# A retention recurrence and an MLP mixer on one core: four decay tables as steps of their own, a first decay held to land later in the plan, the maxima of the wide product allowed on two engines, and a new written-out order

## The chip, the cores and the metric

The kernel runs on one core of a Trainium2 chip. The metric is the device time of one execution in microseconds (us); the time before is the median of three executions. The engines are named as the profile names them: PE (matrix products; PEld is its weight load), DVE (vector), ACT (scalar), POOL and SP. POOL issues the loads, SP the transposes that are done by DMA, and SP and ACT the stores.

## What is computed

```python
def _attn_ref(q, k, v):                       # q, k, v: [4, 8, 768, 64]
    gamma = 1.0 - 2.0 ** (-5.0 - np.arange(H))
    for t in range(S):
        state = gamma * state + k[:, :, t] (outer) v[:, :, t]
        y[:, :, t] = scale * q[:, :, t] @ state

def _moe_ref(x, w_tok1, w_tok2, w_ch1, w_ch2):  # x: [4, 768, 512] = the heads side by side
    xt = x.transpose(0, 2, 1)
    h = np.maximum(xt @ w_tok1, 0.0) @ w_tok2   # 768 -> 256 -> 768
    u = x + h.transpose(0, 2, 1)
    h2 = np.maximum(u @ w_ch1, 0.0) @ w_ch2     # 512 -> 1536 -> 512
    return u + h2
```

## The kernel before

The work is cut by batch b (four) and, within a batch, by pair p of heads (four). `front(b, p)` does the recurrence and the token mixing of a pair; `back(b)` does the channel mixing of a batch.

A front works on six chunks of 128 positions. `decayed` multiplies k (and, for late pairs, q) by powers of the decay into `k16` and `q16`; there are two of these multiplies for a tile, one for each head, and each may go to ACT or DVE. `turn` transposes: mode "t" by PE (L348) with a copy to `kT` (L361), mode "w" by PE (L346) with a DVE multiply by the table `gq` into `qT` (L356), mode "x" by a DMA transpose from SP (L336). L377 makes the state products k'v, the chain of L387 and L389 scans them on DVE into `U`, and L398 or L401 scales the states into `r16`. L417 makes the scores k'q, L427 masks them on DVE (four times 384 wide for a pair), L438 and L447 add up y, L453 casts it. L467, L476 and L487 are the token mixing with the weights `wt1` and `wt2`; L493 casts u to fp16, L503 copies u to the tile `X`, and `uT` gets its transpose, by PE (L533, L540) in batch 0 and one pair of batch 1 and by a DMA transpose from SP (L517) otherwise.

`back` has two halves. Batches 0 and 1 widen plainly: L571 multiplies 384 positions at a time, and L587 takes the maximum while it leaves the bank. Batches 2 and 3 use a seven-product scheme (`widen7`): L612 makes sums of `uT`, L644 the products, L656 keeps partial sums on ACT, L661 adds on DVE, L682 and L690 take the maxima. L690 handles two 384-wide pieces at once in SBUF. All batches narrow with `narrow7`: L749 makes sums of the widened tiles, L785 and L795 are the products, L775 keeps, L802 adds into `X`, and the rows of `X` are stored (L832).

Tiles rotate through a few buffers: four each for the loads of q, k and v, and three for `X`, so batch 3's `X` takes the buffer of batch 0's.

The order is written out: nothing is scheduled when the kernel is built. The string PLAN names every step by two characters, in the order in which they are emitted; a further character chooses the engine where a step has several (`either`), and one the PSUM bank. `+n` stands for n products of a zero tile (L906) that fill PE. Each engine and each queue works its own steps in this order. The costs in the code (`act`, `dve`, and the pairs of numbers in `one` and `either`) served the search that wrote the string; at run time only the string counts.

The preparation makes tables: `gk` and `gy`, `ident16`, `gq` (four exponentials, one a pair, L222, in one step), `gs`, `gp` (on POOL, L232 and L234), `mask`. The first k tile, `(0, 0, "k")`, is called hard: it is loaded in fp32 by SP, not by POOL, and its two decay multiplies read fp32.

Of the kernel before, what the change touches and what calls it, by code (L numbers as in the profile page):

```python
# [9 lines left out]
F16 = mybir.dt.float16  # L10
# [11 lines left out]
class Op:  # L22
# [18 lines left out]
    "04050b000f010d0c0g03020e1h11i00907+e1n4061j51o1p1l10a2r01k11R01m+32v50i2w0h1q1r1s2s11S11u26+91v411x0j2t31T01w1"  # L41
    "U01V51z08+31A01W1y0l1X10k1Y2452260m1t01B1Z1D42u0+125651E31027+32x22820293203360n2y0p2z212A+23531C0340222B0q362"
    "C2F511F02a60r2302I2D0+22d32b2e0o2J2E251G12H1H2N51I02G2K22L3f712M02c11J1K01L01M2f12O3i3j1N12g73711O00s2P12h1P43"
    "8393a3H02i00z3b1Q03c2j0u2m2k03I2l03D12Q42n03n12R3e072S03E13h2p62T0t2W0x3F73d02U00y3g3k02q12o12V03l3o3G12X04f60"
    "v3m04g3p02Z33q43012Y03r0A3s14b03Q65273Rah33t3U3w4c0ae63S3T3u03z43x04d73B3A13J53C1af4e0agai4J13y03v13K4K13LaO4a"
    "R7aSaPaj3Man60E3NaQ3Y2ao4L0ak4aT3OaC53P10waDalapaEaU73V63WaV3Z4M1aW4P04h10B3X1400aI74iam0DaL54QaJ414424RaX34S0"
    "CaMaK4304T4U4j4kaYaZ441d451aF4aG47az7aN1baA460aw5191eaBat65h1axauaH4lbf4ay1fbg4mav5i00H1a1c4o10530I4804N6aq7ar"
    "4pbhbi4bjas4sb334904Obk4q5j14rb44W26045k14n0b07b654Y4t1b10Gb54V0bo504ub2bl6bp4Z4v0bmb74w34xbc7bn4z0151gbu64a4X"
    "4y0bvb84A164B0544b9555bd0F5Q0ba51252be4F4Cbs7bq1817bb5300Kbr4D0bKbt05704G0bO55604H00L4E05R0bxbwbLby158bz65n3bM"
    "5W15o5900PbP0bA0M5X5l0bB5a5T05p5YbT5U05ZbNbD5b06r05dbC0bU05m60bGbX5q5rbE61bH5V5e0ca65sc65f00S5Sc75u1043bY06s0c"  # L50
    "b1cc75yc2bV35vcd6o0c35x6p00JcfbQ55t05w5C05z4bWc8cg00O0N5A7u10R6t5D620bRbZc95B0c05c0cj5F7c15E0ck14I5G631523bS65"
    "645H0co5I5L5J06667ch55K1cp6870Q69ci6u26b45M06a06c5g5O36e16v6d16q6wclbF6f6x5N06y5P06g06zcT3cs6cmct6W1cU6kcu6B02"
    "51cV6E0Wc50cE66A1cF6D6X0d23d3cG6h7v0cN5cO6Fcv6cw7x10Td4db2cx6CcP6J16Z1cQ3bI0cR6G0cH5cScIdc6K6i16Hcecn6l16j0726"
    "c41dd7017A76Y6m0cy2cK3czcJ8A17y07Bd547CcL0V7D6I173cAd8571cr0dw2dxd60X7EcM7FcZ7d7dyd96L074cW3d00Yd17z6M2cX7w756"
    "N76da7G0dh4cB777cCdq6dr6O08B0781de5cYcDbJ0di820dk2dldjdf6Pdsdn7dCdt3dm0UdodpdudgdDdz4dA8318CdFdvdG2796735dEdBd"
    "H1dN46Q06n6S7c6T0dL6R17ddO7a6V7b6U0e23dM0dY850dRdP7e6dQ08D0dS7H01758E07fdU7g08617h47ie0847K0Ze97e307j07L7J7k11"
    "47P57Q7l7IeadVdTed877M07N7m113dZeee18827O08G17n8H7R0898F8a7q7o07r08b7S77T8c7p08I8J8de7dI67U08K7Y7s08LdJe80ek12"
    "el7Vem7W0eb8f41267Z0818i80011ec0eo77t8g7X0ep18jev58M0e44et8h8N0126e5enew8Re6egeh8Pez8k4ef8n68e0eu08QeA9b08l8oe"
    "x8m08Oeq38q18p08rey0eC9G08S0ercq18s09808T9H18teK39c0eG8u0eD8weY78V1eM5eL8x08WeBdKeHeZ8v08y0991eIeNeJes10eOf29M"
    "49e69I9Nf028U09f8Y58X08Zf1ePf3eR9gf5eQ2900eS9194f69O9h9ieW9PeT9j9Qfc9dff5eUf46920eXfgfa950fh3fj9k1fb9R9J1f7ft4"  # L60
    "fkfdf8fv79aej1960eVfu930fmfif9fwfnfl2fx9l0136frfyfA9K0fK7fBfLfo9ofsfpfHfz3fF9pfqg06fCfY5fZfO9n9mfDfPfIfM2g2fGg"
# [34 lines left out]
def kernel(  # L96
# [123 lines left out]
    def emit():  # L220
        for p in range(NP):
            nc.scalar.activation(gq[:, p], SINCE.tile.rearrange("p a b -> p (a b)")[:, :SH], AF.Exp, bias=lnsc, scale=lnh[:, p:p + 1])  # L222
# [716 lines left out]
```

## Time and profile before

| | |
|---|---|
| median of three executions | 187.66 us (187.24 to 189.37) |
| the profiled execution | 188.25 us, of it 186.5 us span from its first to its last instruction |
| busy, of the span | PE 178.7, DVE 164.9, ACT 122.6, POOL 53.4 us |
| DMA | 25.51 MB, 94377 packets |

The profile is of one execution. PE's busy time holds the modelled end of each matmul, which overlaps the next one; the distance between the starts says more than the busy time. "Idle before" in a row is the time in which the engine stood still ahead of these instructions, with what released it.

### The profile page before, as it was taken

What the parts mean: (1) busy time and instruction counts of PE and PEld (TensorE: products, weight loads), DVE (VectorE), ACT (ScalarE), POOL (GpSimd) and SP (SyncE); (2) the same over time, 40 slices, a digit from 0 to 9 for tenths busy, and PEclk for the clock granted to TensorE, in tenths of its full rate; (3) what the DMA queues carried; (4) which work ended last, traced back from release to release, by engine and by line L of the source; (5) the groups of instructions that cost most, each with busy time, mean ns of one, the idle gap of its engine ahead of it and who ended that gap; (6) DMA issues with size and microseconds to landing.
All of it is one profiled execution on the core that took longest, in us unless ns stands there. A gap on an engine that the chain in (4) does not pass through costs nothing.

```text
span 186.5 us, 5228 instructions
## 1 busy us (share of the span) xinstructions
PE 178.7 (96%) x2083; PEld 135.6 (73%) x2083; DVE 164.9 (88%) x433; ACT 122.6 (66%) x284; POOL 53.4 (29%) x65
## 2 busy tenths in 40 slices
PE   7987999999999999999999999999999999999991
PEld 3554788676678988866668988875688986667880
DVE  3798999868999998989259999999999999799992
ACT  3668588857879775677885586999793425773220
POOL 8996775455422008902000750000000000000000
PEclk9999999999999999999999999999999999999999
DMA  8999999999999979999993999880533040511045
GB/s 117 163 159 196 179 175 191 179 193 205 178 162 150 137 78 131 181 182 194 158 218 65 114 148 134 143 189 22 88 98 102 37 118 10 218 62 54 4 158 182
DMA packets 94377, 25.51 MB, mean 137 GB/s; under 512 B 84368, under 2 KB 91536, under 8 KB 94352
## 3 DMA queue, kind: packets, MB, share of 16 engines
q0 software_dynamic: 67456, 13.18, 90.6%
q1 hardware_dynamic: 25168, 9.11, 26.6%
q10 hardware_dynamic: 1728, 2.88, 4.5%
q8 instruction: 16, 0.26, 0.6%
q14 instruction: 9, 0.07, 0.1%
HBM read 26.74 MB, written 6.29 MB: 177 GB/s over the span
## 4 chain that ended last, share of the span: by engine, by line
PE 82%; DMA 7%; DVE 6%; POOL 1%; issue 1%; ACT 1%; DVEq 0%; POOLq 0%
PE bank L571 17%; PE bank L644 15%; PE bank L785 15%; PE bank L795 11%; DMA q<-in_q_dram 7%; PE bank L487 6%; PE bank L467 5%; PE bank L417 3%; DVE X L802 3%; PE bank L438 3%; PE bank L447 2%; PE bank L346 1%; PE bank L377 1%; PE bank L533 1%; DVE hs L749 1%; DVE qT L356 1%
## 5 line engine op out<-in xcount | busy, mean ns | idle before, releaser
L571 PE MATMUL bank<-uT,wc 128*128 128x384 f16 x192 | 35.6, 326 | 0.2 <-DVE uT L540 0.2
L427 DVE TENSOR_TENSOR am<-bank,mask 128x384 f16<-128x384 f32 x64 | 32.8, 548 | 1.0 <-PE bank L417 0.9
L284 POOL DMA_DIRECT2D v<-in_v_dram x16 | 16.7, 1043 | 42.8 <-PE bank L447 22.1
L587 ACT ACTIVATE h<-bank 128x384 f16<-128x384 f32 x48 | 22.0, 494 | 8.4 <-PE bank L571 8.0
L571 PEld LDWEIGHTS <-wc 128*128 128x128 f16 x192 | 17.4, 98 | 9.7 <-DVE uT L540 0.2
L785 PEld LDWEIGHTS <-hs 128*128 128x128 f16 x216 | 20.4, 98 | 3.5 <-DVE hs L749 0.5
L775 ACT COPY us<-bank 128x256 f32<-128x256 f32 x29 | 10.6, 378 | 18.8 <-PE bank L785 18.2
L661 DVE TENSOR_TENSOR h<-bank,us 128x384 f16<-128x384 f32 x36 | 18.7, 550 | 1.7 <-PE bank L644 0.9
L785 PE MATMUL bank<-wsum,hs 128*128 128x256 f16 x144 | 19.5, 273 | 0.0
L656 ACT COPY us<-bank 128x384 f32<-128x384 f32 x36 | 16.4, 489 | 4.6 <-PE bank L644 3.7
L802 DVE TENSOR_TENSOR X<-X,bank 128x256 f32<-128x256 f32 x48 | 19.0, 412 | 0.1
L389 DVE SCALAR_TENSOR_TENSOR U<-U,gs,bank 128x64 f32<-128x64 f32 x64 | 16.5, 277 | 1.1
L284 POOL DMA_DIRECT2D k<-in_k_dram x15 | 15.4, 1035 | 6.6 <-ACT u L493 2.4
L493 ACT CAST u<-bank 128x384 f16<-128x384 f32 x27 | 12.5, 483 | 5.6 <-PE bank L487 5.3
L453 ACT CAST x<-bank 128x384 f16<-128x384 f32 x25 | 11.6, 489 | 6.3 <-PE bank L447 6.3
L795 PEld LDWEIGHTS <-h 128*128 128x128 f16 x144 | 13.7, 98 | 1.8 <-DVE am L427 0.2
L644 PE MATMUL bank<-hs,wsum 128*128 128x384 f16 x72 | 14.8, 326 | 0.0
L467 PE MATMUL bank<-x,wt 128*128 128x128 f16 x192 | 14.5, 219 | 0.1
L749 DVE TENSOR_TENSOR hs<-h 128x768 f16<-128x768 f16 x20 | 10.9, 551 | 3.7 <-ACT h L587 3.7
L487 PE MATMUL bank<-h,wt 128*128 128x128 f16 x192 | 14.2, 219 | 0.0
L802 DVE TENSOR_TENSOR X<-X,us 128x256 f32<-128x256 f32 (+1 forms) x25 | 13.0, 534 | 0.6 <-ACT x L453 0.5
L487 PEld LDWEIGHTS <-wt 128*128 128x128 f16 x192 | 12.1, 98 | 1.5
(86 smaller groups left out, 361.2 us busy)
## 6 DMA issues: line engine op xcount, KB each, us to landing
v<-in_v_dram POOLq DMA_DIRECT2D x16, 192.0 KB, 9.2
q<-in_q_dram POOLq DMA_DIRECT2D x16, 192.0 KB, 8.6
out_dram<-X SPq DMA_DIRECT2D x12, 256.0 KB, 2.4
k<-in_k_dram POOLq DMA_DIRECT2D x15, 192.0 KB, 8.5
wc<-in_moe_w_ch_dram POOLq DMA_DIRECT2D x5, 512.0 KB, 13.4
out_dram<-X ACTq DMA_DIRECT2D x10, 256.0 KB, 2.4
wt<-in_moe_w_tok_dram POOLq DMA_DIRECT2D x2, 384.0 KB, 8.9
wc<-in_moe_w_ch_dram POOLq DMA_DIRECT2D x2, 256.0 KB, 10.1
```

The costliest lines, as they stand in the source:

```text
L284: (nc.sync if hard else nc.gpsimd).dma_start(out=s.tile, in_=src.rearrange("h (c p) d -> p h c d", p=P))
L389: nc.vector.scalar_tensor_tensor(out=u[:, c], in0=u[:, c - 1], scalar=gs[:, p:p + 1], in1=st, op0=ALU.mult, op1=ALU.add)
L427: nc.vector.tensor_tensor(am, SC[g].tile[:, :m * P].rearrange("p (i t) -> p i t", t=P), mask.to_broadcast([P, m, P]), ALU.mult)
L467: nc.tensor.matmul(acc[:, jt * P:(jt + 1) * P], wt1[:, i, jt * P:(jt + 1) * P], X16.tile[:, i], start=(i + jt == 0), stop=(i == NC - 1), s ...
L487: nc.tensor.matmul(Y[hf].tile[:, i * P:(i + 1) * P], wt2[:, jt, t], H1.tile[:, jt], start=False, stop=(jt == NJ - 1), skip_group_check=True)
L571: nc.tensor.matmul(acc[:, :SH], wc1[:, ct, ft * P:(ft + 1) * P], UT.tile[:, ct, sh * SH:(sh + 1) * SH], start=(ct == 0), stop=(ct == NP - 1))
L587: nc.scalar.activation(H2.tile[:, ft], A.tile[:, :SH], AF.Relu)
L644: nc.tensor.matmul(acc[:, :SH], left(ct), r[:, ct], start=first and ct == 0, stop=ct == 1, skip_group_check=True)
L661: nc.vector.tensor_tensor(into(hf)[:, ft], bank.tile[:, :SH], kept(j), ALU.add)
L785: nc.tensor.matmul(acc_[:, lo], l[:, j], r[:, j], start=first and j == 0, stop=j == K2 - 1, skip_group_check=True)
L795: nc.tensor.matmul(acc_[:, lo], l[:, j], r[:, j], start=first and j == 0, stop=j == K2 - 1, skip_group_check=True)
L802: (nc.vector if e == "DVE" else nc.gpsimd).tensor_tensor(dst(), dst(), b_(), ALU.add)
```

## The change

Four edits in the code, and a new string.

1. The step that makes the four tables `gq` becomes four steps, and each q turn waits for its own table alone.
2. The DVE cost of the hard decay is put at 800 to 900 in place of 335 to 420. This number is not read at run time; it is one of those from which the order was made.
3. In the last pair of batch 0, the two halves of the transpose of u get a bank each.
4. The maxima over two pieces in `widen7` may go to ACT as well as to DVE.

```diff
-    def emit():
-        for p in range(NP):
+    gq_ops = []
+    for p in range(NP):
+        def emit(p=p):
             nc.scalar.activation(gq[:, p], SINCE.tile.rearrange("p a b -> p (a b)")[:, :SH], AF.Exp, bias=lnsc, scale=lnh[:, p:p + 1])
-    gq_op = prep("ACT", 2490, emit, [since_op, lnh_op, lgs_op], (-20, 0, -1, 1), uses=[SINCE])
+        gq_ops.append(prep("ACT", 622, emit, [since_op, lnh_op, lgs_op], (-20, 0, -1, 1), uses=[SINCE]))
...
-                got.append(op(either(emit, ACT=(506, 610), DVE=(335, 420) if hard else (232, 312)),
+                got.append(op(either(emit, ACT=(506, 610), DVE=(800, 900) if hard else (232, 312)),
...
-                return op(one("DVE", (870, 950), emit), [t, gq_op], [dst], [T])
+                return op(one("DVE", (870, 950), emit), [t, gq_ops[p]], [dst], [T])
...
-            qt = turn(Q, QT, ql, "x")
+            qt = turn(Q, QT, ql, TURN[b, p, "q"])
...
-            T, t = Slot(FA), None
+            t = None
             for lot in ([0], [1]) if last else ([0, 1],):
                 c0, c1 = lot[0] * HC, lot[-1] * HC + HC
+                T = Slot(FA)
...
-                        def emit(hf=hf, ft=ft):
+                        def emit(e, hf=hf, ft=ft):
                             h = H[hf].tile[:, ft:ft + 2]
-                            nc.vector.tensor_scalar(h, h, 0.0, None, ALU.max)
-                        rel[hf][ft] = rel[hf][ft + 1] = op(one("DVE", (265, 350), emit), [rel[hf][ft], rel[hf][ft + 1]],
+                            if e == "ACT":
+                                nc.scalar.activation(h, h, AF.Relu)
+                            else:
+                                nc.vector.tensor_scalar(h, h, 0.0, None, ALU.max)
+                        rel[hf][ft] = rel[hf][ft + 1] = op(either(emit, DVE=(265, 350), ACT=act(2 * SH, sbuf=1)), [rel[hf][ft], rel[hf][ft + 1]],
                                                            [], [H[hf]])
```

The string is new from its first character. Read step by step, the two strings hold the same steps, apart from the three more for `gq`, and the same products on PE. They differ in order, in engines and in the filling products (37 before, 39 after; 14 and 17 of them ahead of the first real product). In the lists below a number such as k02 is batch 0, pair 2.

| | before | after |
|---|---|---|
| loads on POOL, in order | v00 q00 q02 k02 k01 q01 v01 k03 v02 (gp) q03 wt1 wt2 v03, q10 k10 q11 wc1 k11 k12 v10 wc1 wc1 ... | v00 q00 k01 k02 (gp) q01 q02 v01 q03 wt1 v02 k03 wt2 v03, k10 q10 q12 k11 q11 wc1 v10 v11 wc1 wc1 ... |
| first steps of ACT | gk gy, k00, gq (all four), k02, k01, copy of kT01, r00 | gk gy, k00, gq of pairs 2, 0, 1, copy of kT00, k01, gq of pair 3, k01, k02, copy of kT01, r00 |
| ahead of the second token product (L487) of pair 00, on PE | all of pairs 00 and 01 up to there, the turns of 02 and 03, the scores of 02 and half of those of 03, y of 02 (both L438, one L447) | the same without half the scores of 03 and without y of 02 |
| the maxima over two pieces | 18 on DVE | 13 on DVE, 5 on ACT |
| stores | 14 on SP, 12 on ACT | 19 on SP, 7 on ACT |
| on SP around the last transposes of batch 2 | uT of 23, uT of 22, the last store of batch 0 | a store of batch 1, uT of 22, uT of 23, three stores of batch 0 |

Of the steps that may go to either engine, DVE gives up, net: five maxima, four keeps (L775), three copies to `uT`, two casts of y, two token maxima (L476, L478) and a copy to `kT`; it takes on, net, six decay multiplies, one scaling of the states (L401) and two casts of u. The edit of `turn(Q, ...)` changes nothing by itself, since that branch only meets pairs whose entry is "x".

More of the change, by code (lines that the diff above doesn't have):

```diff
@@ L46 @@
[L46 to L55, printed above, removed]
@@ L66 @@
[L66 to L68 removed]
+    "0500040e010i0a021k01l1080603+h1q60g0h1r0j1s0c1t070b1u1m01n0+21o21p+61y041x120d1U01A091v1B1C1V0+51W62u01Y51z0f+"
+    "11D41Z0l2y11X027061w01E28352022z2v00o2a0n2c29+42w5386211F01G12b2x022391H+21J50m232I361I0240k0p1K2M1L0252602A02"
@@ new lines @@
+    "L3400q2B2d52C2g32H622D2e2h2J2f03510t2E+23662F1M2K2i03711P0s0z2j73i062k2G01N11O01Q03m3a43l3b3h261R03c2Q12l02N03"
+    "G12O3H13k0v2R2P02S03d3j2m2n00u2o02p3I73e2q02T63f2U3n23g10r3J11S50x2s42V03q62W3r1T02r02Z0y2X12Y03o4Q74e12t03K34"
+    "i53p13s00w3003t43u3103203v04f14R4g73303w3z3L3x04j3T04313X3y04h03Wak53A03C23B13M13N0D4k73D0ah33E2al3O3Vaian6aja"
+    "q44l3F1aoaramapaU53PaR33U3Y2as3QaV3R0C4maSb06aT4naW3S1b10A4o0J411aX44p3Z0H0B4M1aC50GaDb97bab334q0b44N1aYb2aE40"
+    "11g4O04450KaZ42aO6b5aP1c430bi3bb0F0E4P10IaQbj45bk460aI75o04Z4563aJ475k01h0LaK1j5p514a504S01d48053aL5aMaz74TaA5"
@@ L69 @@
+    "jFjpj90jO6jC1jbjN0jcjZ1jdjf1j2jB1j3jQjPjGjR0jejg1jSjTjUjVjWjXk01jY0k10"
 )
```

50 lines of the change are left out of this document (26 added, 24 removed).

## The prediction

> **What bounds the kernel now.** I read the page first, for the engine that carries the end, then a table by stretches, to see where that engine stands still.
>
> ```profile
> span 186.5 us, 5228 instructions
> PE 178.7 (96%) x2083; PEld 135.6 (73%) x2083; DVE 164.9 (88%) x433; ACT 122.6 (66%) x284; POOL 53.4 (29%) x65
> PE 82%; DMA 7%; DVE 6%; POOL 1%; issue 1%; ACT 1%; DVEq 0%; POOLq 0%
> ```
>
> The third line is the chain of waits: 82% of it is PE. Then the stretches; the first number after the length of one is PE's busy time, and the first behind the five engines the granted clock.
>
> ```profile
> 6.00:12.00 6.00, 5.30 (x74) 3.27 (x70) 4.92 (x13) 2.77 (x5) 5.88 (x11) 1.00 1.94 162
> 12.00:18.00 6.00, 4.94 (x80) 2.97 (x76) 5.75 (x17) 5.04 (x10) 4.81 (x6) 1.00 1.87 182
> 18.00:24.00 6.00, 5.61 (x107) 4.48 (x108) 5.36 (x12) 3.67 (x9) 3.94 (x5) 1.00 1.75 183
> 24.00:182.00 158.00, 157.47 (x1813) 122.42 (x1810) 145.26 (x363) 107.97 (x257) 33.38 (x35) 1.00 1.18 132
> ```
>
> From 24 to 182 us PE is idle for 158.00 - 157.47 = 0.5 us; a faster DVE or ACT can win no more than that there, though a late one can cost any amount. From 6 to 24 us PE is idle for 0.70 + 1.06 + 0.39 = 2.15 us, and part of its busy time is filling. The granted clock is 1.00 throughout. So the change can win in the first 24 us, and lose anywhere.
>
> The head, in order of time:
>
> ```profile
> 1.12 4.66 PE L906 MATMUL bank<-zero 128*128 128x384 f16 x14 [1.12 <-DVE zero L899]
> 5.71 0.48 PE L377 MATMUL bank<-v,k 128*64 128x64 f16 x10
> 6.88 0.53 PE L346 MATMUL bank<-ident,q 128*64 128x128 f16 x12 [0.25 <-DMA q<-in_q_dram]
> 7.34 0.66 PE L906 MATMUL bank<-zero 128*128 128x384 f16 x3
> 8.53 0.34 PE L417 MATMUL bank<-qT,kT 64*128 64x128 f16 x6
> ...
> 13.14 0.34 PE L438 MATMUL bank<-v,am 128*128 128x64 f16 x6
> ...
> 18.07 0.53 PE L346 MATMUL bank<-ident,q 128*64 128x128 f16 x12 [0.94 <-DMA q<-in_q_dram]
> ...
> 21.44 0.66 PE L438 MATMUL bank<-v,am 128*128 128x64 f16 x12
> 21.93 0.28 PE L447 MATMUL bank<-r,qT 128*128 128x128 f16 x2
> 22.14 0.34 PE L417 MATMUL bank<-qT,kT 64*128 64x128 f16 x6
> 22.42 0.84 PE L487 MATMUL bank<-h,wt 128*128 128x128 f16 x12
> ```
>
> Fourteen fills, the first products at 5.71, first y at 13.14, a wait for q03 until 18.07 (0.94 on PE), and the token product L487 of pair 00 at 22.42. I use this last one as the milestone.
>
> **The change part by part.** *Three more fills at the start.* Fourteen took 4.66 us (0.33 each); the later three took 0.66 (0.22 each with the tail). Three more cost 0.5 to 1.0; I take 0.6 for what lies between, so L377 starts at 6.3. What hides it is the wait for q00, which landed at 6.88; without that cover it costs itself.
>
> *The first pair.* I follow the new order with these durations:
>
> ```profile
> 5.05 2.48 ACT L222 ACTIVATE gq<-us,lnsc,lnh 128x384 f32<-128x384 f32 x4
> ...
> L427 DVE TENSOR_TENSOR am<-bank,mask 128x384 f16<-128x384 f32 x64 | 32.8, 548 | 1.0 <-PE bank L417 0.9
> L398 ACT ACTIVATE r<-U,gp 128x320 f16<-128x320 f32 x24 | 12.1, 564 | 0.9 <-DVE U L389 0.9
> L322 ACT ACTIVATE k<-k,gk 128x384 f16<-128x384 f16 x17 | 10.2, 621 | 3.4 <-DMA k<-in_k_dram 3.4
> L356 DVE TENSOR_TENSOR qT<-bank,gq 128x768 f16<-128x768 f16 x8 | 7.6, 952 | 1.3 <-PE bank L346 1.3
> L690 DVE TENSOR_SCALAR h<-h 128x768 f16<-128x768 f16 x18 | 6.0, 353 | 0.1
> L361 ACT COPY kT<-bank 128x768 f16<-128x768 f16 x4 | 3.2, 795 | 1.2 <-PE bank L348 1.2
> ```
>
> The four tables took 2.48, so 0.62 each; three of them end at 5.05 + 1.86 = 6.9, before kT00 is wanted at about 7.3, and the copy ends at 8.1. Split tables therefore win nothing by themselves for pair 0, whose table was not late before either. The q turn of pair 00 starts at about 7.6 behind two fills, DVE multiplies from 8.1 to 9.05, and both halves of the scores (0.34 each) run at once from 9.1, where before nine fills stood between them. Four masks of 0.55 and a scan step of about 0.2 follow from 9.45 to 11.8. So y of pair 00 starts at 11.8 against 13.14.
>
> *The loads.* A landing is set by how many loads stand ahead:
>
> ```profile
> 7.71 1.07 POOL L284 DMA_DIRECT2D k<-in_k_dram  x1
> DMA to landing us min/median/max: 7.3/7.3/7.3
> ```
>
> This is k03, the eighth load on POOL, which landed at 15.0. The eleventh, the first token weights, landed at 19.4, so 1.5 a load:
>
> ```profile
> 11.00 0.86 POOL L260 DMA_DIRECT2D wt<-in_moe_w_tok_dram  x1
> DMA to landing us min/median/max: 8.4/8.4/8.4
> 9.96 0.42 POOL L234 COPY gp<-gs 64x4 f32<-64x4 f32 x2
> ```
>
> In the new order q03 is the eighth, the token weights the ninth and k03 the eleventh, with the same eleven loads in all. So q03 is there at 15.0 instead of 18, the weights at about 16.5, k03 at 19.4 instead of 15.0. The table gp is moved up on POOL past five loads. It issues no transfer and waits only for gs, which DVE now makes before the first k lands; its two copies held POOL for 0.42, small beside loads that are issued 7 us ahead of their landing.
>
> *The milestone.* The turn of q03 goes at about 15.3, the first token product at 16.5. The states of pair 01 are scaled on ACT (two of 0.564) until about 19.4; one half of k03 follows there (0.62, to 20.0), the other on DVE to 20.5; PE turns k03 at 20.6 and comes to L487 at 20.95. Ahead of it there is less work than before: y of 02, one L447 and half the scores of 03, which fill 21.44 to 22.42 in the rows above, 0.98 us, come later. At equal work the new order is at 21.93, 0.5 us ahead of 22.42. This is the gain I expect. Its bounds: the walk may be wrong by a load's 1.5 us to the bad side, or the whole 2.15 us of idle time goes.
>
> *After the head.* DVE has eight steps fewer, five of them maxima. PE had 0.5 us of idle time from 24 us on, so a lighter DVE wins 0 to 0.5; I take 0, since a new order has stalls of its own. The five at 0.353 take 1.8 us off DVE. On ACT the nearest row is a 768-wide copy, 0.795, so 4.0 us more, or up to 1.24 each if two passes of the 384-wide 0.62 are nearer; what hides them is ACT's idle third. The bank for each half of uT03 takes away one wait in one place: 0 to 0.2, taken as 0. Stores moved from ACT to SP cost ACT less issue time; what is queued behind them on SP is the second rival.
>
> *A rule that speaks against this.* The Trainium skill, ScalarE: Activation LUTs, section "Rules for kernel authors", says to put max and relu on VectorE, up to about three times faster there on 16-bit data. The trace agrees in direction: 0.353 against 0.795, a little over twice. What it would do to the time is the third rival, worked out there from rows.
>
> *The end.*
>
> ```profile
> 181.66 0.82 PE L785 MATMUL bank<-wc,hs 128*128 128x256 f16 x6
> 182.41 1.00 ACTq L832 DMA_DIRECT2D out_dram<-X  x2
> ```
>
> Behind the last product stand adds and two half stores, to 186.5. The new order ends in the same way, with one more full store on SP close to the end: 0 to 0.7, taken as 0.
>
> The sum: 186.5 - 0.5 = 186.0 of span. The profiled execution took 188.25, so 187.75 by it; the median is 0.59 lower than this execution, and against it the forecast is 187.66 - 0.5, about **187.2**. A change of 1% is about what a measurement of this kernel can tell from none.
>
> **The rivals.** *All the idle time of the head goes.* Every load is then in time for its product. Gain: 2.15, and 0.3 of the 0.5 later; 187.66 - 2.45 = 185.2, faster by 1.3%. For it: q03 and the token weights come earlier, the two waits that the head shows. Against it: in my walk k03 and the chain on ACT end last, not PE.
>
> *ACT waits for stores.* The first copy to `X` of batch 3 (L503) needs batch 0's buffer, so all six stores of batch 0 must have landed.
>
> ```profile
> 110.85 2.55 SPq L517 DMA_TRANSPOSE uT<-u  x2
> 113.45 1.68 SPq L832 DMA_DIRECT2D out_dram<-X  x1
> 121.12 0.91 ACT L503 COPY X<-bank 128x384 f32<-128x384 f32 x2
> ```
>
> Before, one store came on SP behind the two last transposes of batch 2, at 113.45, and L503 at 121.12: 6 us to spare. After, a store of batch 1 that waits for DVE goes ahead of the transposes, which stand about 2 us later in PE's order, and three stores of batch 0 behind them. At 1.68 each they are issued by 113.45 + 2 + 3 x 1.68 = 120.5, and a landing is due before 121.12. If the landing takes over 0.6 us, ACT stands, and with it the casts of u and the keeps (L656) that PE waits for. With 2 to 4.5 us of it reaching PE: 189.2 to 191.2, say 190. It decides from the point where ACT waits longer than the 1.6 us of token products and other work that PE has there. Against it: in the quick case a store's issue is far shorter than 1.68, as the code's own order reckons.
>
> *ACT becomes the bound of the wide product*, the mechanism of the quoted rule. In batch 3 a maximum on ACT stands ahead of ACT's last keep and last two single maxima, for which L749 waits. One such maximum costs 0.8 there, if ACT has no slack: 187.2 + 0.8 = 188.0. Of this stage the stretches say
>
> ```profile
> 160.00:170.00 10.00, 10.00 (x68) 6.44 (x67) 8.93 (x22) 7.15 (x17) 0.00 (x0) 1.00 0.26 99
> ```
>
> ACT (7.15 of 10) has 2.85 us left, more than two maxima need; so it is not likely.
>
> **How the numbers follow.** Forecast (a small gain from the head) 0.43, ACT as the bound 0.08, all the idle time gone 0.20, stores 0.29. The first two are within 1% of 187.66 (185.8 to 189.5): 0.51. Faster 0.20, slower 0.29. The forecast's own range is 186.2 to 188.7: half of 2.15 gained, or a load late by 1.5. For eight in ten I take 185.2, the first rival's value, to 190.3, which is the second's with a little above it.
>
> **What would show it.** Right: L377 at about 6.3, y of 00 near 11.8, q03's turn near 15.3, L487 of pair 00 near 21, and PE idle by less than 1 us from 24 us to the end. Wrong: L487 behind 22 with a wait for DMA or ACT ahead of it; a wait of ACT ahead of L503 near 120 us, with PE idle behind it; or waits of L571 near 30 to 36 us, since the second block of channel weights has one more load ahead of it (1.5 us), which I priced at nothing.

## The result: 0.5% slower, where 0.3% faster was forecast

| | before | after |
|---|---|---|
| median, same chip, 20 runs each | 187.75 us (187.06 to 189.37) | 188.89 us (188.30 to 190.41) |
| ratio after to before | | 1.0053, 95% interval 1.0035 to 1.0071 |
| the profiled execution | 188.25 us, span 186.5 | 188.78 us, span 187.0 |

The change costs 1.1 us between medians, and 0.5 us between the two profiled executions. The difference between these two numbers is part of the answer: the profile of before is of an execution 0.5 us over its median, the one of after is 0.1 under it.

The page of the kernel after, first line, busy times and the shares of the chain of waits:

```profile
span 187.0 us, 5243 instructions
PE 179.4 (96%) x2085; PEld 136.2 (73%) x2085; DVE 164.0 (88%) x425; ACT 126.5 (68%) x291; POOL 53.4 (29%) x65
PE 80%; DVE 14%; issue 1%; ACT 1%; DVEq 0%
```

PE's share of the chain is nearly as before. VectorE's share went from 6% to 14%, though VectorE has eight instructions fewer. This is the first sign: not how much VectorE works, but when.

The table by stretches of the kernel after (columns as in the prediction):

```profile
6.00:12.00 6.00, 5.75 (x75) 3.38 (x73) 4.09 (x11) 4.40 (x8) 6.00 (x9) 1.00 1.95 166
12.00:18.00 6.00, 5.46 (x91) 3.53 (x90) 5.75 (x12) 3.57 (x7) 4.11 (x5) 1.00 1.85 178
18.00:24.00 6.00, 5.27 (x96) 4.13 (x95) 5.75 (x17) 4.94 (x12) 4.57 (x6) 1.00 1.76 183
24.00:182.00 158.00, 157.28 (x1811) 122.41 (x1811) 144.26 (x355) 110.55 (x261) 33.50 (x35) 1.00 1.18 132
```

From 6 to 24 us PE is idle for 0.25 + 0.54 + 0.73 = 1.52 us, where it was 2.15. From 24 to 182 us it is idle for 0.72, where it was 0.5. So the head got better and something later got worse. The rows that the prediction named, in order of time:

```profile
6.68 0.48 PE L378 MATMUL bank<-v,k 128*64 128x64 f16 x10
...
12.47 0.35 PE L439 MATMUL bank<-v,am 128*128 128x64 f16 x6 [0.18 <-DVE am L428]
...
15.68 0.53 PE L347 MATMUL bank<-ident,q 128*64 128x128 f16 x12
...
21.22 0.83 PE L488 MATMUL bank<-h,wt 128*128 128x128 f16 x12
```

Line numbers are one to five higher after (L487 is L488, L785 is L790, L795 is L800, L802 is L807, L832 is L837, L775 is L780, L690 is L695 on VectorE and L693 on ScalarE). In the kernels that mix the two orders the later ones are one lower again (L789, L799, L806). VectorE is DVE in the rows and ScalarE is ACT.

Where the lead is lost is seen in the last products, which are the same in both kernels. Four of the last five, before and then after:

```profile
179.04 0.82 PE L795 MATMUL bank<-wsum,hs 128*128 128x256 f16 x6
179.70 0.82 PE L785 MATMUL bank<-wc,hs 128*128 128x256 f16 x6
180.35 0.82 PE L785 MATMUL bank<-wsum,hs 128*128 128x256 f16 x6
181.01 0.82 PE L795 MATMUL bank<-wsum,h 128*128 128x256 f16 x6
```

```profile
178.74 0.82 PE L800 MATMUL bank<-wsum,hs 128*128 128x256 f16 x6
179.39 0.82 PE L790 MATMUL bank<-wc,hs 128*128 128x256 f16 x6
180.05 0.82 PE L790 MATMUL bank<-wsum,hs 128*128 128x256 f16 x6
181.29 0.81 PE L800 MATMUL bank<-wsum,h 128*128 128x256 f16 x6 [0.42 <-DVE X L807]
```

At the first of them the kernel after leads by 0.30 us. At the fourth it is 0.28 behind, since that product waits for an addition on VectorE. The step of 0.58 us is the 0.42 of the row and the modelled end of the product ahead of it. What VectorE does around it:

```profile
173.44 0.41 DVE L780 COPY us<-bank 128x256 f32<-128x256 f32 x1
...
180.03 0.41 DVE L807 TENSOR_TENSOR X<-X,bank 128x256 f32<-128x256 f32 x1
180.48 0.42 DVE L807 TENSOR_TENSOR X<-X,us 128x256 f32<-128x256 f32 x1
180.82 0.41 DVE L807 TENSOR_TENSOR X<-X,bank 128x256 f32<-128x256 f32 x1
181.15 0.55 DVE L754 TENSOR_TENSOR hs<-h,hs 128x768 f16<-128x768 f16 x1
```

The addition that PE waits for is the one at 180.82; additions of the pair of rows (0, 1) stand ahead of it, the last of them at 180.48. At 173.44 there is a bank copy, which the kernel before has on ScalarE. VectorE's last additions, before and then after:

```profile
182.30 0.74 DVE L802 TENSOR_TENSOR X<-X,bank 128x256 f32<-128x256 f32 x2
```

```profile
182.62 0.74 DVE L807 TENSOR_TENSOR X<-X,bank 128x256 f32<-128x256 f32 x2
```

They start 0.32 us later, and from there to the end of the span it is 4.4 us where it was 4.2. These two make up the 0.5 us between the profiled executions.

### The profile page after: what moved, and what is told of

Read it like the earlier page. It is cut to its first block, busy times and chain, and to the rows that moved or that the text cites. A ratio compares the mean times of both kernels' runs of the same rounds, so it can differ in the third digit from the quotient of the medians.

```text
span 187.0 us, 5243 instructions
## 1 busy us (share of the span) xinstructions
PE 179.4 (96%) x2085; PEld 136.2 (73%) x2085; DVE 164.0 (88%) x425; ACT 126.5 (68%) x291; POOL 53.4 (29%) x65
## 4 chain that ended last, share of the span: by engine, by line
PE 80%; DVE 14%; issue 1%; ACT 1%; DVEq 0%
PE bank L573 17%; PE bank L646 13%; PE bank L790 13%; PE bank L800 10%; PE bank L488 6%; PE bank L468 5%; DVE X L807 4%; PE bank L418 3%; PE bank L439 3%; PE bank L911 3%; DVE hs L754 3%; PE bank L448 2%; DVE am L428 2%; PE bank L378 2%; DVE h L663 2%
## 5 line engine op out<-in xcount | busy, mean ns | idle before, releaser
L573 PE MATMUL bank<-uT,wc 128*128 128x384 f16 x192 | 36.4, 326 | 0.0
L428 DVE TENSOR_TENSOR am<-bank,mask 128x384 f16<-128x384 f32 x64 | 32.4, 547 | 1.4 <-PE bank L418 1.3
L780 ACT COPY us<-bank 128x256 f32<-128x256 f32 x33 | 12.3, 381 | 20.0 <-PE bank L790 20.0
L790 PEld LDWEIGHTS <-hs 128*128 128x128 f16 x216 | 20.5, 98 | 2.5
L658 ACT COPY us<-bank 128x384 f32<-128x384 f32 x36 | 16.9, 484 | 4.8 <-PE bank L646 3.9
L807 DVE TENSOR_TENSOR X<-X,bank 128x256 f32<-128x256 f32 x48 | 19.2, 412 | 1.0 <-PE bank L800 0.9
L790 PE MATMUL bank<-wsum,hs 128*128 128x256 f16 x144 | 19.5, 273 | 0.0
L390 DVE SCALAR_TENSOR_TENSOR U<-U,gs,bank 128x64 f32<-128x64 f32 x64 | 17.8, 282 | 1.1
L800 PEld LDWEIGHTS <-h 128*128 128x128 f16 x144 | 13.6, 98 | 2.9 <-issue 0.9
L488 PE MATMUL bank<-h,wt 128*128 128x128 f16 x192 | 14.7, 219 | 0.0
L454 ACT CAST x<-bank 128x384 f16<-128x384 f32 x27 | 12.5, 486 | 2.6 <-PE bank L448 2.3
L504 ACT COPY X<-bank 128x384 f32<-128x384 f32 x27 | 13.3, 495 | 0.8 <-DVE u L494 0.7
L494 ACT CAST u<-bank 128x384 f16<-128x384 f32 x25 | 11.9, 489 | 2.8 <-PE bank L488 2.8
L807 DVE TENSOR_TENSOR X<-X,us 128x256 f32<-128x256 f32 (+1 forms) x25 | 13.2, 533 | 0.2
```

The source lines that it names most:

```text
L390: nc.vector.scalar_tensor_tensor(out=u[:, c], in0=u[:, c - 1], scalar=gs[:, p:p + 1], in1=st, op0=ALU.mult, op1=ALU.add)
L428: nc.vector.tensor_tensor(am, SC[g].tile[:, :m * P].rearrange("p (i t) -> p i t", t=P), mask.to_broadcast([P, m, P]), ALU.mult)
L488: nc.tensor.matmul(Y[hf].tile[:, i * P:(i + 1) * P], wt2[:, jt, t], H1.tile[:, jt], start=False, stop=(jt == NJ - 1), skip_group_check=True)
L573: nc.tensor.matmul(acc[:, :SH], wc1[:, ct, ft * P:(ft + 1) * P], UT.tile[:, ct, sh * SH:(sh + 1) * SH], start=(ct == 0), stop=(ct == NP - 1))
L790: nc.tensor.matmul(acc_[:, lo], l[:, j], r[:, j], start=first and j == 0, stop=j == K2 - 1, skip_group_check=True)
L800: nc.tensor.matmul(acc_[:, lo], l[:, j], r[:, j], start=first and j == 0, stop=j == K2 - 1, skip_group_check=True)
```

## The experiments

All moves are moves in the written-out order; a token such as `j01` is one step and the engine chosen for it. Kernels that mix the two orders start from the code after, but keep the bank for both halves of uT03 as before, so that both orders hold the same steps. The medians are of 4 to 12 executions (4 of maxima_back, 6 of new_head, tail_mended, old_head and head_undone). The ratio is to the kernel before in runs beside them; for the kernel after it is 1.0053 (1.0035 to 1.0071).

| kernel | median us | before beside it | ratio (95%) |
|---|---|---|---|
| new_head | 190.86 | 187.84 | 1.0174 (1.0143 to 1.0205) |
| new_half | 188.31 | 187.84 | 1.0028 (1.0010 to 1.0046) |
| old_tail | 188.39 | 187.84 | 1.0018 (1.0001 to 1.0035) |
| one_add | 188.91 | 187.84 | 1.0062 (1.0040 to 1.0084) |
| maxima_back | 190.01 | 187.90 | 1.0114 (1.0093 to 1.0136) |
| copy_on_act | 188.57 | 187.90 | 1.0036 (1.0017 to 1.0055) |
| old_from_135 | 188.02 | 187.90 | 1.0019 (1.0001 to 1.0038) |
| tail_mended | 189.68 | 187.72 | 1.0092 (1.0067 to 1.0118) |
| before_two_max | 187.84 | 187.72 | 1.0002 (0.9985 to 1.0019) |
| fewer_fills | 188.80 | 187.72 | 1.0049 (1.0031 to 1.0068) |
| old_head | 195.71 | 187.72 | 1.0394 (1.0355 to 1.0432) |
| head_alone | 189.02 | 187.78 | 1.0065 (1.0036 to 1.0095) |
| head_undone | 189.77 | 187.78 | 1.0117 (1.0074 to 1.0159) |
| end_undone | 187.63 | 187.78 | 1.0006 (0.9979 to 1.0033) |
| end_alone | 189.35 | 187.78 | 1.0072 (1.0042 to 1.0103) |
| stores_on_act | 188.31 | 188.02 | 1.0021 (1.0001 to 1.0040) |
| stores_and_copy | 188.07 | 188.02 | 1.0001 (0.9979 to 1.0022) |

**The orders cut apart, first try.** Three kernels take the first steps from the new order and the rest from the old.

```diff
 PLAN (new_head: n = 252; new_half: n = 785; old_tail: n = 1175)
 the first n steps of the new order
-the rest in the new order
+the rest in the order of before
```

> The kernel before in every step, except that the first 252 of its 1250 planned steps (fillers counted among them; the start and the first three pairs' fronts, up to about 30 us) stand in the new order, with four decay tables in place of one step; all maxima on VectorE, stores as before. Theory (the new head gains what the traces show at equal TensorE work, 0.7 to 0.85 us, and the order behind it loses it): 186.9 to 187.1 us, ratio to the kernel before 0.996. Rival (the lead is taken up by a wait behind the head whatever the order there): 187.5 to 187.9, ratio 1.000. Rival (the new head is itself what is slow, and the traces mislead since they are one execution each): 188.3 or more, ratio 1.003 or above.

> The first 785 planned steps (up to about 110 us) in the new order, the rest in the order of before, so that the maxima on two engines and the new end are left out. Theory (of the lead of 0.85 us some 0.5 is lost between 45 and 105 us of the span, and the rest in the last 15 us): 187.2 to 187.5 us, ratio 0.998. Rival (all is lost in the first half): 188.3 or more, ratio 1.003 or above. Rival (nothing is lost in the first half): 186.9, ratio 0.996, as for the new head alone.

> The first 1175 planned steps in the new order (maxima on two engines with them), and the last 75, from about 170 us on, in the order of before, with the late stores that this moves to the queue of before. Theory (the new end alone costs 0.5 to 0.6 us): 188.3 us, ratio 1.002 to 1.003. Rival (the end is worth nothing, since the middle sets the time): 188.9, ratio 1.005. Rival (the whole loss beyond the head's lead lies in the end): 187.3 or less, ratio 0.998 or less.

new_head is 3 us above all that the theory and the first rival allow; only the last rival, open upwards (188.3 or more), takes it in. Its trace shows why, a wait at the join for a v tile that the rest of the old order wants sooner than the new loads bring it:

```profile
43.14 0.35 PE L378 MATMUL bank<-v,k 128*64 128x64 f16 x10 [2.21 <-DMA v<-in_v_dram]
```

In new_half PE waits for 0.52 us at its join (114.39 us), in old_tail for 0.65 at 170.49. So a cut is only of use where the two orders have done nearly the same, and the numbers of these three bound things from one side: with the old end, and a wait of 0.65 at the join on top, old_tail is still 0.5 us faster than the kernel after. So the end costs something like that or more; the intervals of the two ratios leave it 0.3 us of play to either side. For the first half new_half decides nothing: it stands at the lower edge of the rival "all is lost in the first half" (188.3), and without its join wait between that and the theory.

**One addition moved.**

```diff
 one_add, VectorE's order
-jc ... j2 ... j3 ... jP    (additions of (0, 1), then the one PE waits for)
+jP jc ... j2 ... j3 ...
```

> The changed kernel with one VectorE addition moved: the one (L807) that the TensorE product at 181.29 us waits for stands ahead of three additions of the pair (0, 1) and of one other there, not behind them. Theory (that wait of 0.42 us is on the path that sets the end): 188.4 to 188.6 us, ratio to the kernel before 1.003. Rival (the stores on SP set the end, and the additions that now come later hold them up): 188.9 to 189.2, ratio 1.005 or above.

No change (188.91), which is the rival's value. The rival's reason, that the stores on SP set the end, is not needed for it: in the trace PE no longer waits for the addition but, at 181.92, 0.41 us for the sum (L754) that stands in the same queue. The wait changed its name, not its size.

**Maxima and copy.** Two kernels change one kind of engine choice in the kernel after.

```diff
 maxima_back
-fh1 fM1 gh1 iS1 ip1     (five maxima on ScalarE)
+fh0 fM0 gh0 iS0 ip0     (on VectorE)
 copy_on_act
-j01                     (bank copy at 173.44 on VectorE)
+j00                     (on ScalarE)
```

> The changed kernel with its five ScalarE maxima (L693, three in batch 2 and two in batch 3) on VectorE again, at the same places in the order. Theory (from 165 us on VectorE is the engine that sets the end: it is busy without a break, and the last TensorE products wait for it): the two of batch 3 come back to VectorE with some 0.27 us each, so the end moves by about 0.5 us and the time is 189.3 to 189.5 us, ratio to the kernel before 1.008. Rival (ScalarE is the bound of the wide product, and its 0.86 us maxima hold up the copies): 188.3 or less, ratio 1.003 or less. Rival (neither: TensorE alone sets the end): 188.9, ratio 1.006.

> The changed kernel with one bank copy of the last wide sum (L780, 0.41 us on VectorE at 173.44 us) on ScalarE, as the kernel before has it. Theory (VectorE sets the end): one VectorE instruction with a step of 0.34 us fewer, so 188.5 to 188.6 us, ratio to the kernel before 1.004. Rival (the waits of TensorE or the stores set it): 188.9, ratio 1.006.

Both came out on the side of the theory. Without the copy the median falls by 0.32 us, about one VectorE step of 0.34; by the medians alone that is within the intervals (1.0017 to 1.0055 against 1.0035 to 1.0071). In the trace the same product now waits less:

```profile
180.39 0.82 PE L790 MATMUL bank<-wsum,hs 128*128 128x256 f16 x6
181.37 0.81 PE L800 MATMUL bank<-wsum,h 128*128 128x256 f16 x6 [0.16 <-DVE X L807]
```

The traces say more when they are counted from a product near the start that all kernels of this kind reach in the same order, so that what lies behind it differs by the change alone. Here it is the group of token products at 58 us, after and then copy_on_act:

```profile
57.87 0.50 PE L468 MATMUL bank<-x,wt 128*128 128x128 f16 x6
```

```profile
58.27 0.50 PE L468 MATMUL bank<-x,wt 128*128 128x128 f16 x6
```

This execution of copy_on_act was 0.40 us late by then, for reasons of its first loads. From this group on, in us, with the three kernels that follow further below:

| kernel | the group | last additions on VectorE | from the group to them | to the end of the span |
|---|---|---|---|---|
| after | 57.87 | 182.62 | 124.75 | 129.1 |
| one_add | 57.83 | 182.78 | 124.95 | 129.3 |
| copy_on_act | 58.27 | 182.70 | 124.43 | 128.7 |
| maxima_back | 58.11 | 184.10 | 125.99 | 130.2 |
| tail_mended | 57.75 | 182.64 | 124.89 | 129.4 |
| stores_on_act | 58.08 | 182.86 | 124.78 | 128.5 |
| stores_and_copy | 58.12 | 182.57 | 124.45 | 128.2 |

So the copy is worth 0.32 us at the last additions, as in the medians.

With the maxima back on VectorE the time rises by 1.1 us, twice what two steps of the last batch explain. The waits of PE in that trace after 100 us sum up to

```profile
PE bank L800 <- DVE X L807: 0.7, 2, 0.4
```

of which 0.4 is in the trace of after too. The rows place the rest. At 137 us maxima_back stands 0.33 behind after (137.64 and 137.31); at this group of products, after and then maxima_back, 1.00:

```profile
141.33 0.82 PE L800 MATMUL bank<-wc,h 128*128 128x256 f16 x6
```

```profile
142.33 0.81 PE L800 MATMUL bank<-wc,h 128*128 128x256 f16 x6
```

That is 0.67 us at the end of batch 2's wide product, where three of the five maxima stand; there VectorE's masks (L428) start at 140.33, not at 139.34. The two of the last batch add the rest, between 167 and 174 us.

**The old order from 135 us on, and a second profile of before.**

```diff
 old_from_135
 the first 965 steps of the new order
-the rest in the new order
+the rest in the order of before
```

> The first 965 planned steps (up to about 135 us) in the new order, the rest in the order of before with all maxima of that rest on VectorE. Theory (the new order has lost nothing up to there, and the whole loss against the kernel before is made from 150 us on): 187.5 to 187.9 us, ratio 0.998 to 1.001. Rival (the head itself loses against a typical run of before): 188.3 to 188.7, ratio 1.003 to 1.005. A join that fits badly would show as a new TensorE wait near 135 us and is then to be taken off.

> The kernel before, once more, for a second profile of it, since its first stands at 188.25 us, 0.5 above its median. Theory (those 0.5 us lie in the first 30 us, where the order waits for its first loads): TensorE reaches the work it had done at 30 us some 0.3 to 0.5 us sooner than in the first profile, and the rest runs alike. Rival (they lie in the stores at the end): the last VectorE addition stands at the same time as in the first profile.

old_from_135 is 0.9 us faster than the kernel after: most of the loss is made behind 135 us. It stands between theory and rival. before_again took 188.27 us. Its first 14 us differ from those of the first profile (L377 at 5.96, the first q turn at 7.50), but from 15 us on it shows the same rows within 0.1 us, with a wait of 1.08 us for q03. So it didn't tell where the 0.5 us over the median lie; another run did, below.

**Mending the end, and the old kernel with two maxima moved.**

```diff
 tail_mended, on copy_on_act
-jc ... j2 ... j3 ... jP jG
+jP jG jc ... j2 ... j3 ...
 before_two_max, on the order of before
-two maxima of the last batch on VectorE; sum n0[0] ahead of n0[2]
+both on ScalarE, behind a keep and behind the last single maximum; n0[2] ahead of n0[0]
```

> The changed kernel with the bank copy on ScalarE, as in copy_on_act, and with the addition that the product at 181.3 us waits for and the last sum of the pair (4, 5) both ahead of the two additions of the pair (0, 1). Theory (VectorE's sum of work sets the end, its order hardly): as copy_on_act or at most the 0.16 us better that its trace still shows as a TensorE wait, 188.4 to 188.6 us, ratio to the kernel before 1.003. Rival (the order of VectorE's queue sets the end): 188.1 or less, ratio 1.001 or less.

> The order of before with two of the nine maxima of the last batch on ScalarE, where ScalarE is idle (near 167.4 and 169.3 us), and one sum of the pair (0, 1) ahead of another. Theory (VectorE, busy without a break from 163 us on, sets the end in the kernel before too): two steps of 0.27 us fewer on VectorE, 187.2 to 187.5 us, ratio to the kernel before 0.997 to 0.998. Rival (TensorE sets the end there): 187.8, ratio 1.000. Rival (ScalarE's 0.86 us maxima hold up the copies and the reluctant sums behind them): 188.2 or more, ratio 1.002 or above.

Both theories fell in part. tail_mended takes away PE's wait (its trace has none after 31 us), VectorE stands still for 0.53 us instead. By the table the last additions come 0.46 us later than in copy_on_act, and the end 0.7 later. The additions of (0, 1) now come later, and with them two full stores; the landing times of its last stores (2.7 us) are the longest of all. The median is 1.1 us above copy_on_act; this profile (188.94) is of an execution 0.7 under its median and does not show the rest. In before_two_max the two steps fewer on VectorE are worth nothing: in the order of before VectorE does not set the end, PE does. "VectorE sets the end" is shown for the new order alone.

The trace of before_two_max has a use of its own. Its head is that of before (its four tables stand in a row), and this execution has a span of 185.9, close to the median. Rows of it, then of before:

```profile
17.41 0.53 PE L347 MATMUL bank<-ident,q 128*64 128x128 f16 x12
...
21.95 0.84 PE L488 MATMUL bank<-h,wt 128*128 128x128 f16 x12
...
98.28 0.82 PE L789 MATMUL bank<-wsum,hs 128*128 128x256 f16 x6
```

```profile
98.84 0.82 PE L785 MATMUL bank<-wsum,hs 128*128 128x256 f16 x6
```

The turn of q03 stands at 17.41 with no wait; in before it stood at 18.07 behind 0.94 us of waiting for the load. The token product is 0.47 earlier, and at 98 us the lead is 0.56: what is gained or lost on the first loads stays to the end. The wait for q03 on which the forecast rested belongs to some executions of the old order and not to others: of the six profiles with the old head it is in three (0.94, 1.08 and, in old_head below, 0.91 us) and not in three (before_two_max, head_undone, end_alone). At the first of the last five products, at 179.04 in before and 178.74 in after, this execution of the old order is ahead of both:

```profile
178.49 0.82 PE L799 MATMUL bank<-wsum,hs 128*128 128x256 f16 x6
```

**Fills, and the head the other way round.**

```diff
 fewer_fills
-+h
++e                      (17 starting fills, then 14)
 old_head
-the first 305 steps in the new order
+the first 305 steps in the order of before
```

> The changed kernel with 14 starting fills in place of 17, as before. Theory (the three more are hidden by the loads that the first products wait for): 188.9 us, ratio to the kernel before 1.006. Rival (they hold up the first product, which stood at 6.68 us in the first profile after, against 5.71 before): 188.2 to 188.4, ratio 1.002 to 1.003.

> The first 305 planned steps (up to about 35 us) in the order of before, the rest in the new order. Theory now (between typical runs the new head is worth little, since new-head kernels stand only about 0.35 us ahead of the two profiles of before at equal TensorE work, and those were 0.4 us over their median): 188.8 to 189.1 us, ratio to the kernel before 1.005 to 1.007. Rival (the new head is worth the 0.5 us predicted or the 0.85 us of the first pair of profiles): 189.4 to 189.7, ratio 1.008 to 1.010. A join that fits badly would show as a new TensorE wait near 35 us and is then to be taken off.

The fills are worth nothing that can be told (188.80 against 188.89). old_head has again a join that fits badly, with five waits between 48 and 57 us, the longest 1.69 for a q tile; it says nothing on the head.

**Head and end cut where the orders agree.** At step 429 both orders have done the same work on PE; at step 1084 they differ in one addition and one store.

```diff
 head_alone: first 429 steps new, rest as before      head_undone: the reverse
 end_undone: first 1084 steps new, rest as before     end_alone: the reverse
```

> The first 429 planned steps (up to about 58 us) in the new order, the rest in the order of before; at this step both orders have done the same TensorE work and differ in ten steps. Theory (the head is worth nothing between typical runs): 187.6 to 187.9 us, ratio to the kernel before 1.000. Rival (the head is worth the 0.5 predicted, or the 0.85 that the first two profiles show near 40 us): 186.9 to 187.3, ratio 0.996. A join that fits badly shows as a TensorE wait near 58 us and is taken off.

> The first 429 planned steps in the order of before, the rest in the new order. Theory (the head is worth nothing): 188.8 to 189.0 us, ratio to the kernel before 1.006. Rival (the head is worth 0.5 to 0.85 us): 189.4 to 189.8, ratio 1.009. A bad join is taken off.

> The first 1084 planned steps (up to about 148 us) in the new order, the rest in the order of before with the last batch's maxima on VectorE; the two orders differ there in one addition and one store. Theory (the whole loss against before lies in the last 38 us): 187.6 to 188.0 us, ratio to the kernel before 1.000 to 1.001. Rival (a third of it lies ahead of that, in head and middle): 188.2 to 188.4, ratio 1.003.

> The first 1084 planned steps in the order of before, the rest in the new order with two maxima of the last batch on ScalarE. Theory (the new end alone costs 0.75 us or more: 0.55 of TensorE waiting for VectorE, 0.2 of the stores): 188.5 to 188.9 us, ratio to the kernel before 1.004 to 1.006. Rival (the end costs less than 0.4 us by itself): 188.1 or less, ratio 1.002 or less.

end_undone is at 187.63, level with before (interval 0.9979 to 1.0033): the loss lies in the last 38 us, to within half a microsecond. At the first of the last five products it stands at 178.66, beside 178.49 for the old order in before_two_max: the new order up to 148 us is not ahead there either. The other three have waits at their joins. The one of head_alone:

```profile
75.94 0.34 PE L439 MATMUL bank<-v,am 128*128 128x64 f16 x6 [0.85 <-DVE X L806]
```

189.02 - 0.85 = 188.2, above the rival's 187.3 and the theory's 187.9 too: no gain by the head is seen. head_undone has a join wait of 0.41, which leaves 189.4, the rival's lower edge; by itself it settles nothing, since its trace is of an execution 2 us over its median (191.76). end_alone waits for 0.64 at 164.12, in an execution 0.8 over its median; 189.35 - 0.64 = 188.7 is the theory's value.

**The last stores.**

```diff
 stores_on_act
-jf1 jg1                 (last two full stores of rows (0, 1) on SP)
+jf0 jg0                 (on ScalarE's queue)
 stores_and_copy: these two, and j01 to j00
```

> The changed kernel with the last two full stores of the pair (0, 1) issued on ScalarE's queue, as the kernel before has them, in place of SP's, where six store instructions stand in a row for 4.35 us. Theory (the row on SP costs the 0.2 to 0.4 us by which the end of the span stands farther from the last additions): 188.5 to 188.7 us, ratio to the kernel before 1.003 to 1.005. Rival (the transfers themselves set the end, not the queue that issues them): 188.9, ratio 1.006.

> The changed kernel with those two stores on ScalarE's queue and the bank copy of the last wide sum on ScalarE as well. Theory (both are parts of the new end's cost and add up): 188.2 to 188.4 us, ratio to the kernel before 1.002. Rival (only the copy counts): 188.6, ratio 1.004.

Both gain more than the theory has it: the stores are worth 0.58 us (188.89 to 188.31, where 0.2 to 0.4 was expected), the copy 0.32, both together 0.82, and with both the kernel is level with before. By the ratios to the runs of before beside them (1.0053 for the kernel after, then 1.0021, 1.0036 and 1.0001) it is 0.6, 0.3 and 1.0 us; by the table of traces above 0.6, 0.4 and 0.9. In the views by tensor, for the stores issued from 181 us on, the kernel after and then stores_on_act:

```profile
L837 SPq DMA_DIRECT2D out_dram<-X x2: 332/332/333, 182.1 to 183.1; - x2
L837 ACTq DMA_DIRECT2D out_dram<-X x2: 338/338/339, 182.7 to 183.4; - x2
...
DMA to landing us min/median/max: 2.1/2.6/2.6
```

```profile
L837 ACTq DMA_DIRECT2D out_dram<-X x3: 338/338/338, 182.3 to 183.6; - x3
L837 SPq DMA_DIRECT2D out_dram<-X x1: 332/332/332, 183.3 to 183.3; - x1
...
DMA to landing us min/median/max: 1.8/1.9/2.1
```

The first numbers are the time that issuing takes (0.33 us each), then the first and last start. The last issue is not earlier with the stores on ScalarE's queue (183.6 against 183.4), but a store lands after 1.9 us instead of 2.6. From VectorE's last additions to the end of the span it is 4.38 us after (182.62 to 187.0) and 3.74 in stores_on_act (182.86 to 186.6).

It is tempting to say that the queue sets the landing. The traces speak against it. Of the four stores the late ones are the last three, half stores, and these are issued from the same queues in both kernels (ACT, SP, ACT); of the two that moved, the one issued at 182 us lands after 2.1 us in both, and the one at 180 us later from ScalarE's queue (2.7 us) than from SP's (2.0). And end_alone issues its last stores from the same queues as after, yet its last three land fast:

```profile
L836 ACTq DMA_DIRECT2D out_dram<-X x2: 338/338/338, 184.7 to 185.4; - x2
L836 SPq DMA_DIRECT2D out_dram<-X x1: 332/332/332, 185.1 to 185.1; - x1
...
DMA to landing us min/median/max: 1.8/1.8/1.9
```

What goes with the late landing is another transfer. In after, one packet of 8 KB of a queue that the page calls "instruction" (q14) stands among the packets of these stores, here the DMA view from 184.0 to 184.5 us:

```profile
q1 hardware_dynamic: 128, 0.12, 69.0%
q10 hardware_dynamic: 56, 0.05, 28.5%
q14 instruction: 1, 0.01, 3.8%
```

From 184.5 us on, in slices of 0.06 us, the bytes that move fall to about a sixteenth within 0.4 us and stay there until 185.6, as when one of the 16 DMA engines is left with its share:

```profile
GB/s 328 328 393 263 148 49 16 33 16 33 0 33 16 33 16 33 0 0 0 0 0 0 0 0 0 0 0 0 0 0 0 0 0 0 0 0 0 0 0 0
```

In stores_on_act that packet comes only after 185 us, behind nearly all bytes of the stores. So it is throughout: in the eight profiles whose last three stores land after 2.4 to 2.7 us (after, one_add, copy_on_act, maxima_back, tail_mended, fewer_fills, head_undone, old_head), the last such packet starts 2.9 to 3.3 us ahead of the end of the span; in the twelve in which they land after 1.7 to 2.0 us it starts 1.6 us ahead or later. The eight are also those whose SP works the longest list of instructions (94 in the trace, 82 to 91 in the others). That moving two stores off SP moves this packet out of the way is therefore the likely cause of the 0.58 us. No kernel was run that moves the packet alone, so it is not shown.

## Why the prediction was wrong, by its own steps

**The first pair, the loads, the milestone: the walk was right to 0.7 us.** L377 was forecast at 6.3 and came at 6.68, y of pair 00 at 11.8 and came at 12.47, the turn of q03 at 15.3 and came at 15.68, L487 of pair 00 near 21 and came at 21.22. With the 0.98 us of work that comes later, the new order is at 22.20 at equal work, 0.22 us ahead of the profiled 22.42, where 0.5 was forecast. That the wait of the first L571 near 30 to 36 us would grow was named as a danger; it did not.

**The sum: this step failed.** "187.66 - 0.5" takes a gain read off one execution of before and subtracts it from the median of all. The profile stood 0.59 us over the median, and the working carried this along as a constant. It lay, at least for the execution that before_two_max shows, in the very wait for q03 that the change was to shorten: against L487 at 21.95 there, 22.20 at equal work is no gain. Over the medians the head is worth nothing that these runs can tell: end_undone has the whole new head and is level with before, and head_alone is not faster. Between the profiles the lead is 0.30 us at 178.7 us, and the after kernel's span there is near its median while that of before is 0.5 over.

**"The end: 0 to 0.7, taken as 0": this step failed, and it is the larger part.** The text saw "one more full store on SP close to the end" and gave bounds that hold: stores_on_act takes 0.58 us off. The full store itself is not what is late; it lands after 2.1 us in both kernels, and the half stores behind it are late. The text also held that "the new order ends in the same way". It doesn't: a copy of VectorE's is new in the last stage, and additions of (0, 1) stand ahead of the one that PE needs. copy_on_act measures 0.32 us of this.

**"A lighter DVE wins 0 to 0.5; I take 0, since a new order has stalls of its own"** was right in its reason, and should have been followed to the place. Ahead of it the prediction says that a late DVE can cost any amount, but looked for no place where it would be late. In the last 10 us every VectorE step is either ahead of a product or ahead of a store.

**The rivals.** Not all idle time of the head goes: 1.52 of 2.15 us is left. ScalarE does not wait for stores: its copy of batch 3 to `X` stands at 121.61 behind other work, with no idle time ahead of it.

```profile
121.24 0.52 ACT L658 COPY us<-bank 128x384 f32<-128x384 f32 x1
121.61 0.53 ACT L504 COPY X<-bank 128x384 f32<-128x384 f32 x1
```

ScalarE is not the bound of the wide product either; on the contrary, maxima_back loses 1.1 us. The price was near: a maximum on ScalarE takes 0.855 us (0.8 was taken), on VectorE 0.351.

```profile
L693 ACT ACTIVATE h<-h 128x768 f16<-128x768 f16 x5 | 4.3, 855 | 0.0
L695 DVE TENSOR_SCALAR h<-h 128x768 f16<-128x768 f16 x13 | 4.2, 351 | 0.1
```

The rule of the Trainium skill quoted in the prediction (ScalarE: Activation LUTs, "Rules for kernel authors") agrees with these rows on which engine is cheaper, by 2.4 times; to follow it would have cost 1.1 us in this order (maxima_back), where VectorE is the engine that is late. In the order of before, where it isn't, two maxima moved to ScalarE changed nothing (before_two_max, 1.0002).

**Terms at nothing.** Three more fills: nothing that can be told (fewer_fills). The separate banks of uT03 were not tried alone. From 24 to 178 us PE has no more idle time after than before; the answers for PE alone, before and then after:

```profile
24.00:178.00 154.00, 153.47 (x1777) 1.00 1.20 130
```

```profile
24.00:178.00 154.00, 153.70 (x1780) 1.00 1.20 130
```

The time, 188.89, lies in the range given (185.2 to 190.3) and within 1% of the kernel before, the likeliest of the three outcomes; the sign is wrong. That the range holds it is luck: its upper end came from the stores that ScalarE was to wait for, and ScalarE did not wait. The two mended choices at the end take 0.8 to 1.0 of the 1.14 us off the kernel after. They do not give it the end of before. In stores_and_copy, profiled at its median, the last additions start at 182.57 and the span ends 3.8 us later; in before_two_max, the old order close to its median, they start at 181.75 and the end is 4.2 us later. The old order is still ahead on VectorE there and loses part of it behind: in before the last store, issued at 183.1, has landed by 185.0, 1.5 us ahead of the end of the span, where after has 1.0 (issued at 183.4, landed by 186.0, end at 187.0). What sets these last 1.0 to 1.5 us is open, as is the part of tail_mended's time that its profile does not show.

No version that was run beats both kernels: end_undone and stores_and_copy are level with before.

## What to carry to other kernels

Before a wait in a profile is counted as a gain, ask whether it is in every execution: when the profiled run stands over its median by about as much as the gain forecast, the gain may be that excess, and a profile of another execution close to the median settles it. In a new order of work, read the last 10 us apart from all the rest, engine by engine and queue by queue: there nothing hid a step, a copy moved to the busy engine cost its full step, and what lay among the packets of the last stores counted 0.6 us. To compare traces of nearly equal kernels, count from an early product that both reach in the same order: that takes off what the first loads of the one execution did. When two orders are to be compared by parts, cut them where both have done the same work; a cut elsewhere measured the join, not the part: waits of 0.4 to 2.2 us here, and in old_head 4.7 in sum.

## What was not expected of the hardware

Where two 256 KB stores are issued changed when the three half stores behind them land: 2.6 us after their issue with both on SP, 1.8 to 1.9 with both on ScalarE's queue, in otherwise the same kernel. The Trainium skill, DMA: Bandwidth & Descriptors, section "Issuing engines are not separate DMA queues", says that issuing on several engines saves only the sequencer's time to issue. Here the issue times hardly changed (last start 183.4 and 183.6) and 0.58 us of the time did; but end_alone, with the queues of after and landings of 1.8 to 1.9 us, shows that it is not the queue alone. One 8 KB packet of an instruction queue, some 3 us ahead of the end and so among the packets of these stores, goes with all eight late landings; in the twelve others it comes 1.6 us ahead of the end or later.

A wait in the first 25 us was not made good in these traces: the two executions of the old head that differ by 0.47 us at the token product of pair 00 differ by 0.56 at 98 us and by 0.55 at the last products (179.04 and 178.49), since PE has no idle time in between in which to catch up.
